# A mixed attention and convolution kernel: value products of two score slots in one operation, V read back per tile, final inputs loaded early and summed in place

## The chip, the cores and the metric

The kernel runs on one core of one Trainium2 chip. The metric is device time in microseconds (us), smaller is better. Its engines are TensorE (PE in the profile, with its weight loads PEld), VectorE (DVE), ScalarE (ACT) and GpSimd (POOL); SyncE (SP) issues every DMA of this kernel.

## The reference

Two mixers read the same input x (1 x 2048 x 512, bf16) and a gate blends them:

```
g = sigmoid((x * gate_w).sum(-1))
out = g * A(x) + (1 - g) * B(x)

A: 32 heads of 16, 4 segments of 512 tokens. In each segment
   a_dot = softmax(q k^T / 4 + causal mask) v
   a_mem = phi(q) M / (phi(q) z + 1e-6),   phi(t) = t + 1 if t > 0 else exp(t)
   o = sigmoid(beta) * a_mem + (1 - sigmoid(beta)) * a_dot
   M += phi(k)^T v,  z += sum phi(k)         (after the segment)
   A = o @ wo
B: K[d, l] = Re sum_n C dt B exp(dt A l)     (128 states, 2048 lags)
   B = causal convolution of x with K over 2048 tokens, by FFT, + x * D
```

## The kernel before

The kernel is a list of operations that a planner at build time puts into an order for each engine. An operation names its engine, a cost, the tiles that it reads and writes and a key. The planner (`Sched.schedule`, L266) repeatedly lets the engine that can start earliest take, among its operations that are ready within 0.12 us, the one with the lowest key; a copy out of PSUM (`evac`, L254) may go to ACT or DVE, and its key counts `PEN` higher on DVE. DMAs are given a length from their bytes (L251) and stand in SP's list like any operation. On the chip each engine runs its list in order and waits on semaphores. So the keys and costs only set the order; they are written by hand: `KEYS` (L19) spaces the groups of attention, the tables and the tail.

Tiles come from pools at fixed addresses of SBUF. Pools of a later phase lie over those of an earlier one and are given out only when the earlier ones are wholly used up (`blockers`). All eight PSUM banks are shared.

The work, in the order of the keys:

- *Powers* (`ssm_powers`, L800). z = exp(dt A) is squared ten times, so that z^(2^k) exists for k = 0 to 10, each copied to a bf16 tile as re, re, im, -im: two ACT copies (L805, L807), one DVE negation (L809), two ACT squares (L815, L816) and two DVE operations (L817, L818) a level.
- *Attention* (`project`, `group`, `ophase`, `oproj`). For each of 4 segments and 4 head groups of 8 heads there are two `group` calls (L979) of four heads A, B, C, D, 32 in all. A group has five score slots. In a slot PE computes scores transposed, keys on partitions, for two or four (head, key block J) pairs into 1024 columns of two PSUM banks, adds the causal mask by matmuls with an identity, ACT takes the exponential of all 1024 columns (L1012) into a tile `pT`, and PE multiplies it with the values (`g`, L1025). From group `MASKD` on, the mask is a product on DVE instead (L1021). A value product of a head fills 17 of the array's columns, so four heads have a column tile each (`tile_position=(0, 32 * c)`). The slots of A and B and of C and D are separate, except the last one (J = 2), which holds all four heads:

```
slots = [[(Ah, 0, 0, 0), (Bh, 0, 1, 0)],
         [(Ah, 1, 0, 0), (Bh, 1, 1, 0), (Ah, 3, 0, 384), (Bh, 3, 1, 384)],
         [(Ch, 0, 0, 0), (Dh, 0, 1, 0)],
         [(Ch, 1, 0, 0), (Dh, 1, 1, 0), (Ch, 3, 0, 384), (Dh, 3, 1, 384)],
         [(Ah, 2, 0, 0), (Bh, 2, 1, 0), (Ch, 2, 0, 256), (Dh, 2, 1, 256)]]
```

  Block J has 512 - 128 J columns. `ophase` (L1042) transposes and normalizes, `oproj` (L1093) multiplies with wo, scales by the gate and stores rows of the attention part to a scratch tensor `scr_abuf`, 16 stores in all. `gate_tokens` (L878) makes the gate; for the last segment it sends the gate through memory (`scr_gbuf`), and a DVE operation (L896) waits for it.
- *Tables* (`tables`, L1110), four times. Products of the powers (L1138, L1140, L1143) build 20 and 32 factors, whose PE products give the filter K; it goes through memory (`scr_K`).
- *First transform of the convolution input* (`x_level1`), stored to `scr_Z`.
- *Tail* (`tail`, L1192). A loop over 16 tiles t, 3.8 of key apart: the filter's transform, the input's second transform, their complex product on DVE (L1240 to L1244), the inverse transform into V, a copy, and a 256-KB store to `scr_V` (L1258). After every fourth tile 1 MB is read back from it into 32 partitions of `V2` (L1261). Then 16 final sums in four groups of four: a load of x (`xj`) and its product u with D on DVE (L1273), a load of the attention part (`aj`, after all 16 stores of it), three matmuls with an identity and the constant `G2`, and a DVE operation (L1286) that scales, adds `aj` and writes `ou`, which is stored, 512 KB for each group. `xj`, `u`, `aj` and `ou` have two buffers each.

Of the kernel before, what the change touches and what calls it, by code (L numbers as in the profile page):

```python
# [8 lines left out]
BF16 = mybir.dt.bfloat16  # L9
# [6 lines left out]
PEN = 20.0  # L16
MASKD = 24
SHOW = 1
KEYS = (11, 6, 60, 65)  # L19
# [482 lines left out]
def fft_consts():  # L502
# [64 lines left out]
def build_kernel(nc, A_x, A_wq, A_wk, A_wv, A_wo, A_beta, B_A_re, B_A_im, B_B_re, B_B_im,  # L567
                 B_C_re, B_C_im, B_log_dt, B_Dskip, gate_w, out):
    with contextlib.ExitStack() as es:
# [27 lines left out]
        mask01 = cload(pidx[None, :] >= pidx[:, None], "mask01", BF16, 8)  # L597
# [45 lines left out]
        pTP = mkpool("pT", 2048, 7)  # L643
# [12 lines left out]
        pwP = mkpool("pw", 4096, 11)  # L656
# [143 lines left out]
        def ssm_powers(pb, dt, zr, zi):  # L800
            S.tag = "pow"
            A = lambda T: ap(T, n=512)
            for k in range(11):
                pw = Tile(pwP, BF16)
                op("ACT", c_act(1024), lambda e, pw=pw, zr=zr: e.activation(  # L805
                    ap(pw, 0, [[512, 4], [128, 2], [1, 128]]), ap(zr, 0, [[128, 4], [0, 2], [1, 128]]), ACT.Copy), r=[zr], pw=[pw])
                op("ACT", c_act(512), lambda e, pw=pw, zi=zi: e.activation(  # L807
                    ap(pw, 256, [[512, 4], [1, 128]]), ap(zi, 0, [[128, 4], [1, 128]]), ACT.Copy), r=[zi], pw=[pw])
                op("DVE", c_ts4(512), lambda e, pw=pw: e.tensor_scalar(  # L809
                    ap(pw, 384, [[512, 4], [1, 128]]), ap(pw, 256, [[512, 4], [1, 128]]), -1.0, None, ALU.mult), r=[pw], pw=[pw])  # L810
                pws.append(pw)
                if k == 10:
                    break
# [28 lines left out]
        dV = [DT() for _ in range(4)]  # L842
# [136 lines left out]
        def group(s, hg, gi):  # L979
# [3 lines left out]
            slots = [[(Ah, 0, 0, 0), (Bh, 0, 1, 0)],  # L983
                     [(Ah, 1, 0, 0), (Bh, 1, 1, 0), (Ah, 3, 0, 384), (Bh, 3, 1, 384)],
                     [(Ch, 0, 0, 0), (Dh, 0, 1, 0)],
                     [(Ch, 1, 0, 0), (Dh, 1, 1, 0), (Ch, 3, 0, 384), (Dh, 3, 1, 384)],
                     [(Ah, 2, 0, 0), (Bh, 2, 1, 0), (Ch, 2, 0, 256), (Dh, 2, 1, 256)]]
# [3 lines left out]
            seen = {}  # L991
            for si, ent in enumerate(slots):
# [41 lines left out]
                for (hh, J, bk, off) in ent:  # L1034
                    seen[hh] = 1
# [339 lines left out]
```

## Time and profile before

| | |
|---|---|
| three runs, us | 419.36, 419.50, 422.38; median 419.5 |
| the profiled execution | 417.59 us, its span 415.8 us, mean granted clock 0.923 |
| instructions | 8543, of them 3609 matmuls, 589 on DVE, 386 on ACT |
| DMA | 42.06 MB in 41029 packets, mean 101 GB/s |
| longest single waits of engines | PE 12.1 us for `scr_V` at the end; DVE 8.6 us for the gate (L896) |
| wait of ACT's copies (L256) for PE | 54.9 us in 54 waits |

Nearly all matmuls stand under L709, the line of a helper; shapes tell them apart: `128*17` is a value product (128 rows, 17 columns of the array), `32*128` a score product, `128*32 128x20` a table product. L256, L257, L259 and L260 are the copies out of PSUM on ACT and DVE, L252 the DMA issue. A row of a group gives its count, busy time, mean length of one in ns, and the idle time of the engine before it with what ended that.

### The profile page before, as it was taken

What the parts mean: (1) busy time and instruction counts of PE and PEld (TensorE: products, weight loads), DVE (VectorE), ACT (ScalarE), POOL (GpSimd) and SP (SyncE); (2) the same over time, 40 slices, a digit from 0 to 9 for tenths busy, and PEclk for the clock granted to TensorE, in tenths of its full rate; (3) what the DMA queues carried; (4) which work ended last, traced back from release to release, by engine and by line L of the source; (5) the groups of instructions that cost most, each with busy time, mean ns of one, the idle gap of its engine ahead of it and who ended that gap; (6) DMA issues with size and microseconds to landing.
All of it is one profiled execution on the core that took longest, in us unless ns stands there. A gap on an engine that the chain in (4) does not pass through costs nothing.

```text
span 415.8 us, 8543 instructions
## 1 busy us (share of the span) xinstructions
PE 341.9 (82%) x3609; PEld 147.3 (35%) x3609; DVE 310.1 (75%) x589; ACT 297.3 (72%) x386; POOL 3.2 (1%) x9
## 2 busy tenths in 40 slices
PE   4896969899959999999999998488779999982460
PEld 3342313333334543544445442144323334330220
DVE  4889997999547998699953995497626799971283
ACT  4999997988828799889888998299656554841000
POOL 1000000000000000000000000000000000000000
PEclk9998888999979999999999999599889999995595
DMA  8901100021445010010100100156944498577253
GB/s 209 275 31 53 50 0 2 0 77 55 149 121 138 31 52 2 19 18 0 52 2 19 17 2 1 43 216 199 347 121 145 165 253 215 197 198 221 50 150 153
DMA packets 41029, 42.06 MB, mean 101 GB/s; under 512 B 18976, under 2 KB 34464, under 8 KB 40608
## 3 DMA queue, kind: packets, MB, share of 16 engines
q1 hardware_dynamic: 40992, 41.52, 33.8%
q8 instruction: 28, 0.46, 0.5%
q14 instruction: 9, 0.07, 0.1%
HBM read 28.27 MB, written 13.25 MB: 100 GB/s over the span
## 4 chain that ended last, share of the span: by engine, by line
PE 37%; DVE 27%; ACT 19%; DMA 11%; issue 4%; SPq 1%; DVEq 0%
PE psum L709 36%; ACT sb L1012 11%; DVE sb L1143 4%; DVE sb L1140 4%; DVE sb L257 3%; DVE sb L1138 3%; DMA scr_gbuf<-sb 3%; ACT sb L256 2%; DMA sb<-in_A_x_dram 2%; DMA sb<-scr_V 2%; DVE sb L1273 2%; DMA out_dram<-sb 1%; DVE sb L1058 1%; SPq L252 1%; DMA sb<-in_A_wq_dram 1%
## 5 line engine op out<-in xcount | busy, mean ns | idle before, releaser
L709 PE MATMUL psum<-sb 128*32 128x20 bf16 (+13 forms) x3393 | 326.6, 274 | 54.2 <-DMA sb<-scr_V 12.1
L709 PEld LDWEIGHTS psum<-sb 128*32 128x32 bf16 (+4 forms) x3393 | 132.5, 95 | 244.2 <-issue 86.1
L1012 ACT ACTIVATE sb<-psum 128x1024 bf16<-128x1024 f32 x160 | 155.3, 1028 | 11.3 <-PE psum L709 10.4
L256 ACT ACTIVATE sb<-psum 128x512 bf16<-128x512 f32 (+4 forms) x110 | 83.2, 770 | 60.7 <-PE psum L709 54.9
L257 DVE CAST sb<-psum 128x512 bf16<-128x512 f32 (+2 forms) x50 | 45.1, 908 | 36.2 <-PE psum L709 35.7
L1143 DVE TENSOR_TENSOR sb<-sb 128x512 bf16<-128x512 bf16 (+3 forms) x52 | 34.7, 667 | 1.4
L1138 DVE TENSOR_TENSOR sb<-sb 128x512 bf16<-128x512 bf16 (+3 forms) x52 | 35.3, 678 | 0.6
L1140 DVE TENSOR_TENSOR sb<-sb 128x512 bf16<-128x512 bf16 (+3 forms) x52 | 34.9, 672 | 0.0
L1286 DVE SCALAR_TENSOR_TENSOR sb<-psum,sb 128x512 bf16<-128x512 f32 x16 | 11.2, 745 | 19.5 <-PE psum L709 16.2
L259 ACT ACTIVATE sb<-psum,sb 128x512 bf16<-128x512 f32 x27 | 18.3, 691 | 7.2 <-PE psum L709 6.9
L260 DVE TENSOR_SCALAR sb<-psum,sb 128x512 bf16<-128x512 f32 x21 | 15.7, 747 | 4.3 <-PE psum L709 3.5
L1021 DVE TENSOR_TENSOR sb<-sb 128x512 bf16<-128x512 bf16 (+1 forms) x40 | 14.4, 364 | 3.6 <-ACT sb L1012 3.4
L805 ACT ACTIVATE sb<-sb 128x1024 bf16<-128x1024 f32 x11 | 11.7, 1060 | 0.0
L1244 DVE TENSOR_TENSOR sb<-sb 128x1024 bf16<-128x1024 bf16 x16 | 11.1, 692 | 0.6
L1240 DVE TENSOR_TENSOR sb<-sb 128x1024 bf16<-128x1024 bf16 x16 | 11.1, 692 | 0.6
L1058 DVE TENSOR_TENSOR sb<-psum,sb 128x512 bf16<-128x512 bf16 x16 | 11.1, 691 | 0.5
L1242 DVE TENSOR_TENSOR sb<-sb 128x1024 bf16<-128x1024 bf16 x16 | 11.0, 685 | 0.0
L1050 PE MATMUL psum<-sb 128*128 128x128 bf16 x128 | 10.4, 228 | 0.5 <-DVE sb L257 0.2
L1050 PEld LDWEIGHTS psum<-sb 128*128 128x128 bf16 x128 | 8.2, 102 | 4.0 <-ACT sb L256 1.4
L1077 DVE TENSOR_TENSOR sb<-psum,sb 128x256 bf16<-128x256 f32 x24 | 9.1, 419 | 0.3
L1055 DVE RECIPROCAL sb<-psum 128x32 f32<-128x32 bf16 x16 | 5.6, 352 | 4.8 <-PE psum L1050 4.7
L922 DVE TENSOR_SCALAR sb<-psum 128x512 bf16<-128x512 f32 x12 | 8.2, 685 | 1.3 <-ACT sb L921 1.2
(65 smaller groups left out, 143.4 us busy)
## 6 DMA issues: line engine op xcount, KB each, us to landing
sb<-in_A_x_dram SPq DMA_DIRECT2D x12, 512.0 KB, 4.6
sb<-c_D SPq DMA_DIRECT2D x16, 320.0 KB, 3.6
scr_Z<-sb SPq DMA_DIRECT2D x16, 256.0 KB, 2.2
sb<-scr_Z SPq DMA_DIRECT2D x4, 1024.0 KB, 11.1
scr_V<-sb SPq DMA_DIRECT2D x16, 256.0 KB, 2.4
sb<-scr_V SPq DMA_DIRECT2D x4, 1024.0 KB, 7.4
scr_abuf<-sb SPq DMA_DIRECT2D x16, 128.0 KB, 1.9
sb<-scr_abuf SPq DMA_DIRECT2D x4, 512.0 KB, 4.7
```

Source lines behind the costliest of these rows:

```text
L256: fa = lambda e: e.activation(dst(), src(), ACT.Copy)
L257: fd = lambda e: e.tensor_copy(dst(), src())
L259: fa = lambda e: e.activation(dst(), src(), ACT.Copy, scale=scale())
L260: fd = lambda e: e.tensor_scalar(dst(), src(), scale(), None, ALU.mult)
L709: mm = lambda e, o_, l, r_, st, sp, **kw: e.matmul(o_, lhsT=l, rhs=r_, start=st, stop=sp, skip_group_check=True, **kw)
L1012: op("ACT", c_act(1024), lambda e, P=P, pT=pT: e.activation(ap(pT, n=1024), ap(P, n=1024), ACT.Exp, scale=0.25), r=[P], w=[pT])
L1021: op("DVE", c_tt(128 * len(offs)), lambda e, pT=pT, dims=dims: e.tensor_tensor(ap(pT, dims=dims + [[1, 128]]), ap(pT, dims=dims + [[1, 128]]),
L1050: i = e.transpose(ap(P, tb * 256 + gi * 128, n=128), ap(ra[gi], tb * 128, n=128), ap(ident, n=128))
L1058: op("DVE", c_dps(512), lambda e: e.tensor_tensor(ap(o1, dims=[[128, 4], [16, 8], [1, 16]]), ap(P, dims=[[256, 4], [32, 8], [1, 16]]), ap( ...
L1138: op("DVE", c_tt(256 * n), lambda e: e.tensor_tensor(run(tile, ne, dst, 1), run(tile, ne, src, sstep), pwv(0), ALU.mult), r=rd + [pw], w=w ...
L1140: op("DVE", c_tt(256 * n), lambda e: e.tensor_tensor(run(t2, n, 0, 1), run(tile, ne, src, sstep), pwv(1), ALU.mult), r=rd + [pw], w=[t2])
L1143: op("DVE", c_tt(256 * n), lambda e: e.tensor_tensor(D_(), D_(), ap(t2, n * 128, [[-n * 128, 2], [2 * n, 64], [1, 2 * n]]), ALU.add), r=[t ...
```

## The change

The change edits seven things.

1. *Groups.* The five slots become three sets: {A/B block 0, C/D block 0}, {A/B blocks 3 and 1, C/D blocks 3 and 1}, {all heads block 2}. Scores and exponentials stay per slot; both slots of a set write halves of one tile (`pT2`, three buffers; the single tile has one), and there is one mask product and one value operation a set. Its matmuls are sorted so that four heads follow each other. Block 3 now lies ahead of block 1 in its bank.
2. *V.* Every tile is read back by itself after its store: 256 KB into 8 partitions, 16 apart. The rows of `G2` are permuted to match.
3. *Final inputs.* `xj` and `aj` have four buffers each; u is written over `xj`, the sum over its quarter of `aj`; the last group is stored in two halves.
4. *Powers.* Ten levels instead of eleven; the two table steps that used z^1024 are made with z^512 from other factors, the second from the first's result. The copies may go to either engine, and level 0 copies only re and im.
5. *Mask.* `MASKD` 24 becomes 25, so group 24 is masked by matmuls.
6. *Planner.* `PEN` 20 becomes 6.53.
7. *Keys.* New spacings: groups 11 to 11.26, start of attention 6 to 11.5, tables 60 to 60.5 and 65 to 67.9 apart, tail loop 3.8 to 3.16, powers 6 to 10.8, tail start 5 to 43.9 after the tables, `oproj` of a segment from 10 to 16.9 groups after its start.

```diff
-PEN = 20.0
-MASKD = 24
+PEN = 6.53
+MASKD = 25
 SHOW = 1
-KEYS = (11, 6, 60, 65)
+KEYS = (11.26, 11.5, 60.5, 67.9, 3.16, 10.8, 43.9, 16.9)
...
-            G2[4 * tp + i, 0, np.arange(32) * 4 + i] = 2.0 / 4096 * np.cos(ang[:, tp])
-            G2[4 * tp + i, 1, np.arange(32) * 4 + i] = -2.0 / 4096 * np.sin(ang[:, tp])
+            r = 16 * (4 * (tp % 2) + i) + tp // 2
+            G2[r, 0, np.arange(32) * 4 + i] = 2.0 / 4096 * np.cos(ang[:, tp])
+            G2[r, 1, np.arange(32) * 4 + i] = -2.0 / 4096 * np.sin(ang[:, tp])
...
-        pTP = mkpool("pT", 2048, 7)
+        pT2P = mkpool("pT2", 4096, 3)
+        pTP = mkpool("pT", 2048, 1)
...
-        xj2P = mkpool("xj2", 4096, 2, 2)
-        uP = mkpool("u", 4096, 2, 2)
-        ajP = mkpool("aj", 4096, 2, 2)
-        ouP = mkpool("ou", 4096, 2, 2)
+        xj2P = mkpool("xj2", 4096, 4, 2)
+        ajP = mkpool("aj", 4096, 4, 2)
...
-            for k in range(11):
+            for k in range(10):
...
+                if k == 0:
+                    S.evac(lambda pw=pw: ap(pw, 128, [[512, 4], [1, 128]]), lambda zr=zr: ap(zr, 0, [[128, 4], [1, 128]]), 512, r=[zr], pw=[pw], psum16=True)
+                else:
+                    S.evac(lambda pw=pw: ap(pw, 0, [[512, 4], [128, 2], [1, 128]]), lambda zr=zr: ap(zr, 0, [[128, 4], [0, 2], [1, 128]]), 1024,
+                           r=[zr], pw=[pw], psum16=True)
+                S.evac(lambda pw=pw: ap(pw, 256, [[512, 4], [1, 128]]), lambda zi=zi: ap(zi, 0, [[128, 4], [1, 128]]), 512, r=[zi], pw=[pw], psum16=True)
+                if k > 0:
+                    op("DVE", c_ts4(512), lambda e, pw=pw: e.tensor_scalar(
+                        ap(pw, 384, [[512, 4], [1, 128]]), ap(pw, 256, [[512, 4], [1, 128]]), -1.0, None, ALU.mult), r=[pw], pw=[pw])
                 pws.append(pw)
-                if k == 10:
+                if k == 9:
...
+            sets = [[[(Ah, 0, 0, 0), (Bh, 0, 1, 0)], [(Ch, 0, 0, 0), (Dh, 0, 1, 0)]],
+                    [[(Ah, 3, 0, 0), (Bh, 3, 1, 0), (Ah, 1, 0, 128), (Bh, 1, 1, 128)],
+                     [(Ch, 3, 0, 0), (Dh, 3, 1, 0), (Ch, 1, 0, 128), (Dh, 1, 1, 128)]],
+                    [[(Ah, 2, 0, 0), (Bh, 2, 1, 0), (Ch, 2, 0, 256), (Dh, 2, 1, 256)]]]
+            mdims = [[[1024, 2], [512, 2], [1, 128]], [[1024, 2], [512, 2], [1, 256]], [[512, 2], [256, 2], [1, 128]]]
...
+            for si, slots in enumerate(sets):
+                pT = Tile(pT2P if len(slots) == 2 else pTP, BF16)
+                for sj, ent in enumerate(slots):
...
+                    op("ACT", c_act(1024), lambda e, P=P, pT=pT, sj=sj: e.activation(ap(pT, sj * 1024, n=1024), ap(P, n=1024), ACT.Exp, scale=0.25),
+                       r=[P], pw=[pT])
...
+                def g(e, pT=pT, slots=slots, si=si):
+                    ents = [(sj, en) for sj, ent in enumerate(slots) for en in ent]
+                    ents.sort(key=lambda x_: -x_[1][1] if si == 0 else (x_[1][1] != 1))
+                    for sj, (hh, J, bk, off) in ents:
                         c = hh % 4
                         n = 512 - 128 * J
                         i = mm(e, ap(PV, 128 * J, n=n, p0=32 * c, np_=17), ap(vpad[s], J * 544 + (8 * hg + hh) * 17, n=17),
-                               ap(pT, bk * 512 + off, n=n), hh not in sn, J == 2, tile_position=(0, 32 * c))
-                        sn[hh] = 1
+                               ap(pT, sj * 1024 + bk * 512 + off, n=n), si == 0, si == 2, tile_position=(0, 32 * c))
                     return i
-                for (hh, J, bk, off) in ent:
-                    seen[hh] = 1
-                op("PE", 0.32, g, r=[pT, vpad[s]], pw=[PV], key=S.key + 2.5, acq=[raw] if si == 0 else [])
+                op("PE", (0.34, 0.36, 0.24)[si], g, r=[pT, vpad[s]], pw=[PV], key=S.key + 2.5, acq=[raw] if si == 0 else [])
...
-            fm(16, 7, 4, 2, 10)
-            fm(18, 13, 2, 2, 10)
+            fm(16, 13, 2, 2, 9)
+            fm(18, 16, 1, 2, 9)
...
-                S.key = k0 + 4 + 3.8 * t
+                S.key = k0 + 4 + KEYS[4] * t
...
-                S.dma(lambda t=t: bass.AP(Vd, t * 131072, [[1024, 128], [1, 1024]]), lambda V=V: ap(V, n=1024), 262144, r=[V], pw=[dV[t // 4]])
-                if t % 4 == 3:
-                    k = t // 4
-                    S.dma(lambda k=k: ap(V2, n=16384, p0=32 * k, np_=32), lambda k=k: bass.AP(Vd, k * 524288, [[16384, 32], [1, 16384]]),
-                          1 << 20, r=[dV[k]], pw=[V2])
+                S.dma(lambda t=t: bass.AP(Vd, t * 131072, [[1024, 128], [1, 1024]]), lambda V=V: ap(V, n=1024), 262144, r=[V], pw=[dV[t]])
+                S.dma(lambda t=t: sbp(V2, t, 16, 8, [[1, 16384]]), lambda t=t: bass.AP(Vd, t * 131072, [[16384, 8], [1, 16384]]),
+                      262144, r=[dV[t]], pw=[V2], packets=1680)
...
+                u = xj
+                op("DVE", c_f1(2048), lambda e, u=u: e.tensor_tensor(ap(u, dims=[[512, 4], [1, 512]]), ap(u, dims=[[512, 4], [1, 512]]),
+                                                                   ap(dskbT, dims=[[0, 4], [1, 512]]), ALU.mult), r=[dskbT], w=[u], key=k0 + 45)
...
-                    op("DVE", c_dps(512), lambda e, P=P, ou=ou, aj=aj, bl=bl, b4=b4: e.scalar_tensor_tensor(
-                        ap(ou, bl * 512, n=512), ap(P, n=512), ap(omg4T, b4, n=1), ap(aj, bl * 512, n=512), ALU.mult, ALU.add),
-                        r=[P, aj, omg4T], pw=[ou])
-                S.dma(lambda gq=gq: bass.AP(out, gq * 2048, [[8192, 128], [1, 2048]]), lambda ou=ou: ap(ou, n=2048), 524288, r=[ou])
+                    op("DVE", c_dps(512), lambda e, P=P, aj=aj, bl=bl, b4=b4: e.scalar_tensor_tensor(
+                        ap(aj, bl * 512, n=512), ap(P, n=512), ap(omg4T, b4, n=1), ap(aj, bl * 512, n=512), ALU.mult, ALU.add),
+                        r=[P, omg4T], w=[aparts[bl]])
+                nh = 2 if gq == 3 else 1
+                for hh in range(nh):
+                    m = 4 // nh
+                    S.dma(lambda gq=gq, hh=hh, m=m: bass.AP(out, gq * 2048 + hh * m * 512, [[8192, 128], [1, 512 * m]]),
+                          lambda aj=aj, hh=hh, m=m: ap(aj, hh * m * 512, n=512 * m), 524288 // nh, r=aparts[hh * m:hh * m + m])
...
-        S.key = 6.0
+        S.key = KEYS[5]
...
-            S.key = TA0 + GA * (8 * s + 10)
+            S.key = TA0 + GA * (8 * s + KEYS[7])
...
-        tail(TT0 + 4 * TT + 5)
+        tail(TT0 + 4 * TT + KEYS[6])
```

More of the change, by code (lines that the diff above doesn't have):

```diff
@@ L841, in build_kernel @@
         dA = [DT() for _ in range(16)]
-        dV = [DT() for _ in range(4)]
+        dV = [DT() for _ in range(16)]
         dK = [DT() for _ in range(4)]
@@ L1271, in tail @@
                       524288, r=dA, w=[aj], key=k0 + 50)
[L1272 to L1275 removed]
+                u = xj
+                op("DVE", c_f1(2048), lambda e, u=u: e.tensor_tensor(ap(u, dims=[[512, 4], [1, 512]]), ap(u, dims=[[512, 4], [1, 512]]),
+                                                                   ap(dskbT, dims=[[0, 4], [1, 512]]), ALU.mult), r=[dskbT], w=[u], key=k0 + 45)
+                aparts = [aj.part() for _ in range(4)]
+                for a_ in aparts:
+                    a_.wr = list(aj.wr)
                 for bl in range(4):
@@ L1298, in build_kernel @@
         gates()
-        GA, TA0, TT0, TT = KEYS
+        GA, TA0, TT0, TT = KEYS[:4]
         for s in range(4):
```

77 lines of the change are left out of this document (26 added, 51 removed).

## The prediction

> **What bounds the kernel now.** I read the page first, then busy time by stage, then the end of the chain of waits. Page, section 1 (busy us, share of the span, instructions):
>
> ```profile
> PE 341.9 (82%) x3609; PEld 147.3 (35%) x3609; DVE 310.1 (75%) x589; ACT 297.3 (72%) x386; POOL 3.2 (1%) x9
> ```
>
> Busy time by stage (after the stretch and its length: PE, weight loads, DVE, ACT, POOL, granted clock, DMA share, GB/s):
>
> ```profile
> 0.00:308.44 308.44, 262.87 (x3181) 117.58 (x3182) 241.60 (x488) 258.25 (x346) 3.19 (x9) 0.94 0.26 75
> ...
> 20.00:40.00 20.00, 15.82 (x143) 7.42 (x142) 18.48 (x40) 19.88 (x32) 0.00 (x0) 0.95 0.15 52
> 40.00:60.00 20.00, 15.50 (x92) 5.18 (x91) 19.65 (x38) 19.81 (x29) 0.00 (x0) 0.84 0.08 27
> ...
> 160.00:180.00 20.00, 19.44 (x399) 9.95 (x400) 14.47 (x37) 16.65 (x26) 0.67 (x1) 1.00 0.10 17
> 180.00:200.00 20.00, 19.54 (x187) 8.96 (x186) 19.51 (x33) 18.36 (x25) 0.00 (x0) 1.00 0.06 17
> 200.00:220.00 20.00, 18.98 (x230) 9.22 (x227) 13.67 (x34) 17.16 (x21) 0.00 (x0) 1.00 0.04 14
> 220.00:240.00 20.00, 19.77 (x376) 9.78 (x372) 14.27 (x32) 18.42 (x26) 0.00 (x0) 1.00 0.12 19
> ...
> 308.44:378.84 70.40, 66.70 (x380) 25.04 (x380) 53.07 (x83) 39.04 (x41) 0.00 (x0) 0.96 0.65 190
> 378.84:389.80 10.96, 0.00 (x0) 0.00 (x1) 0.00 (x0) 0.00 (x0) 0.00 (x0) 0.50 0.72 205
> 389.80:410.74 20.94, 12.31 (x48) 4.63 (x48) 15.40 (x18) 0.00 (x0) 0.00 (x0) 0.83 0.38 125
> ```
>
> There are four parts. Until 308 us the score groups and the tables run, with PE, ACT and DVE all within 22 us of each other, and the limit changes: ACT at 20 to 60, PE at 160 to 240. Then comes the convolution loop, 70 us on PE; then 11 us in which no engine works; then 21 us of final sums. The end of the chain (start, us, what) says what those last two parts wait for:
>
> ```profile
> 377.79 1.03 ACT sb L256
> ...
> 378.84 3.73 DMA scr_V<-sb
> ...
> 382.58 7.17 DMA sb<-scr_V
> ...
> 389.80 3.70 PE psum L709 x9
> ...
> 394.21 2.27 DVE sb L1273
> 396.47 0.67 DVE sb L1286
> 397.14 0.02 issue
> 397.16 2.83 DMA sb<-scr_abuf
> 399.99 1.99 DVE sb L1286 x3
> ...
> 402.36 5.63 DMA out_dram<-sb
> ```
>
> The last V tile is stored, a quarter of V comes back in one 1-MB read, and the sums then stall on a late product with D, a late load of the attention part and an output store that still holds the buffer.
>
> **The change part by part.** The profiled execution took 417.6 us, of which its span is 415.8; the sum is made against 417.6. The median of the three times shown, 419.5, stands 1.9 above it, and the forecast is given at the median's level.
>
> *Value products.* Five stretches, each one run of value products up to the next matmul's start (the count includes one neighbour at the edge); the first number after the length is PE's time:
>
> ```profile
> 30.12:30.45 0.32, 0.32 (x3) 0.09 (x3) 0.32 (x2) 0.32 (x1) 0.00 (x0) 1.00 0.00 0
> 105.14:105.47 0.33, 0.33 (x7) 0.10 (x7) 0.00 (x0) 0.33 (x1) 0.00 (x0) 1.00 0.85 234
> 139.69:140.23 0.54, 0.54 (x7) 0.20 (x7) 0.51 (x2) 0.54 (x2) 0.00 (x0) 1.00 0.00 0
> 112.51:112.83 0.32, 0.32 (x5) 0.11 (x6) 0.29 (x2) 0.22 (x1) 0.00 (x0) 1.00 0.70 253
> 49.67:49.89 0.22, 0.22 (x5) 0.10 (x6) 0.22 (x1) 0.22 (x1) 0.00 (x0) 1.00 0.00 0
> ```
>
> In order: two heads of 512 alone 0.32; two of 512 with two other heads' 384 and 128 0.33; the same six of only two heads 0.54; four of 384 and 128 on two heads 0.32; four heads of 256 0.22. The second against the third is the heart of it: four column tiles share the time, two do not. Today a group has two products of 512, two of 384 and 128, and one of 256: 4 x 0.32 + 0.22 = 1.50 us if each stands alone, 2 x 0.54 + 0.22 = 1.30 where neighbours on the same heads follow each other. I take the smaller. Changed: all four heads' 512 in 0.32, all four's 384 and 128 in 0.32, and 0.22: 0.86. That is 0.44 us a group and 14.1 us of PE over 32 groups. How much of it reaches the end? Up to 308 us PE (262.9) is ahead of ACT (258.3) by only 4.6. PE is at 19 of 20 us or more only at 160 to 240, a third of the groups' time; elsewhere the saving becomes PE idle time. I take 6.0, somewhat under half. It cannot give more than 14.1. It can also lose: a product now waits for two exponentials, and PE's waits on them, 7.6 us today, might double.
>
> ```profile
> PE psum L709 <- ACT sb L1012: 7.6, 16, 1.5
> DVE sb L896 <- DMA sb<-scr_gbuf: 8.6, 1, 8.6
> ...
> L1012 ACT ACTIVATE sb<-psum 128x1024 bf16<-128x1024 f32 x160 | 155.3, 1028 | 11.3 <-PE psum L709 10.4
> L805 ACT ACTIVATE sb<-sb 128x1024 bf16<-128x1024 f32 x11 | 11.7, 1060 | 0.0
> L807 ACT ACTIVATE sb<-sb 128x512 bf16<-128x512 f32 x11 | 7.0, 633 | 0.0
> L815 ACT ACTIVATE sb<-sb 128x512 f32<-128x512 f32 x10 | 6.3, 628 | 0.0
> ```
>
> *Powers.* One level fewer takes from ACT 1.06 (L805), 0.63 (L807) and two squares of 0.63 (L815 and its twin), 2.95 us; the first level's copy shrinks from 1.06 to 0.63, another 0.43: 3.4 in all. They lie at 20 to 60 us, where ACT is busy 19.9 and 19.8 of 20. DVE is at 18.5 and 19.7 there, so copies that may now go to DVE find little room. I take 2.5, between 0 (hidden) and 3.4 with the 1.7 that DVE loses too (5.1). The table products change exponents but not number or size: 0.
>
> *Masks, order.* One group fewer is masked on DVE and instead needs ten identity matmuls on PE, at 0.1 to 0.2 us 1 to 2 us; DVE gains about as much; 0, bounds 2 either way. The new keys and the lower handicap of DVE in the planner reorder everything; no row prices that. The largest price of one bad place is DVE's 8.6 us on the gate's round trip through memory (L896), whose code and place in the plan stay. I take 0 and 8 either way.
>
> *Attention's output projection of the last segment* gets a key behind the final sums, so PE does it only when it has nothing else: up to 16 matmuls of 512, at 0.26 (142.2 us over 545, row below) 4.2 us, leave the full loop for the 11-us hole. But then the attention part is stored and loaded late. I take 1.5, bounds 4.2 gain and 4 loss.
>
> ```profile
> L709 PE MATMUL psum<-sb 128*128 128x512 bf16 x545 | 142.2, 404 | 24.1 <-DMA sb<-scr_V 12.1 <-issue 5.1 <-DVE sb L257 2.5
> L1286 DVE SCALAR_TENSOR_TENSOR sb<-psum,sb 128x512 bf16<-128x512 f32 x16 | 11.2, 745 | 19.5 <-PE psum L709 16.2 <-DMA out_dram<-sb 3.3
> L1273 DVE TENSOR_TENSOR sb<-sb 128x2048 bf16<-128x2048 bf16 x4 | 9.0, 2282 | 0.0
> ...
> scr_V<-sb SPq DMA_DIRECT2D x16, 256.0 KB, 2.4
> sb<-scr_V SPq DMA_DIRECT2D x4, 1024.0 KB, 7.4
> scr_abuf<-sb SPq DMA_DIRECT2D x16, 128.0 KB, 1.9
> sb<-scr_abuf SPq DMA_DIRECT2D x4, 512.0 KB, 4.7
> out_dram<-sb SPq DMA_DIRECT2D x4, 512.0 KB, 4.4
> ```
>
> *Readback.* 1 MB took 7.17 at the end. A tile is a quarter, but its eight rows are as long as the 32 rows before, so a row's own time stays. Between 2.4 (256 KB, 128 rows) and 7.4 (1 MB) I take 4.6, near the 512-KB loads: gain 2.5, bounds 4.8 and 0. SP issues 16 readbacks instead of 4, each waiting some 2.4 us for its store; behind it stand the next constant loads, which have four buffers, and V stores, which have five: 0 with that cover, a few us without.
>
> The Trainium skill ("DMA: Bandwidth & Descriptors", on how many engines a transfer uses) says that a transfer over eight partitions runs on eight of the sixteen engines, and to keep all sixteen busy. That speaks against this shape, and no row above shows it; spread over sixteen, the readback would be near the 2.4 and the sum about 2 us lower.
>
> *Final sums.* 20.94 us now. With products and attention parts ready and results written in place, the three stalls go. What is left is the first block's three matmuls, 1.2 us (3.70 over 9 at the low clock), 16 sums at 0.70 (11.2 over 16), and 1.0 because the next two blocks' matmuls are as slow and outlast a sum by 0.5 each; with 0.3 for the steps between, 13.7, a gain of 7.2. Bounds: all 15.4 that DVE is busy today stay, 5.5; only PE's 12.3, 8.6. Two products with D of 2.28 each move into the loop, where DVE has 17 us free (53.1 of 70.4): 0; without that cover 4.6. The last store is half as large (4.4 toward 2.4): 0.4, bounds 0 and 2.
>
> Sum: 6.0 + 2.5 + 1.5 + 2.5 + 7.2 + 0.4 = 20.1; 417.6 - 20.1 = 397.5, at the median's level **399.4**. A cross-check up to 308 us: if ACT is the busiest afterwards with 254.9 us, and the busiest keeps today's share (262.9 of 308.4, 85%), that part takes 299, a gain of 9.4 against the 8.5 assumed.
>
> **The rivals.** (a) *Only the end gains.* For it: three engines lie close together up to 308 us, and each waits for the others. Against: PE is full at 160 to 240. Gain 2.5 + 7.2 + 0.4: 419.5 - 10.1 = 409.4. (b) *PE is the bound throughout.* For it: 82% on the page and the whole loop. Then 14.1 of the products, 2.5 of the powers, 4.2 of the projection and 10.1 of the end: 388.6. (c) *The attention part comes late.* After the last loop matmul: 4.2 of projection, 0.7 for its last copy (as long as a sum), 1.9 for the store and 4.7 for a load, 11.5; V is there after 1.0 + 2.4 + 4.6 = 8.0. Four loads of 4.7 then share the queue. If the last sums wait 5 us: 404.4. (d) *Slower: the pairing starves PE.* Each of 64 paired sets waits for a second exponential of 1.03 us. If w of it is uncovered on average, 64w is added; from w = 0.31 the 20.1 are gone. At w = 0.5 the time is 399.4 + 32 = 431.4. For it: the pairs' buffers number three, so PE can run ahead only so far. Against: PE waits on exponentials only 7.6 us today, with tables, projections and convolution input to fill in. (e) *The columns do not overlap*, so the change does not do what it says: 405.4; against it stands the 0.33 run.
>
> **How the numbers follow.** Forecast 0.52, (a) 0.17, (b) 0.15, (c) 0.08, (d) 0.05, (e) 0.03. The range must reach into (b) and over (a): 386 to 411 leaves out (d) and tails of (a) and (b), about 0.15. All but (d) and the far side of (a) are faster by more than 1% (1% is about what a measurement of this kernel can tell from no change): faster 0.90, within 1% 0.05, slower 0.05.
>
> **What would show it.** Right: the four-head 512 run takes about 0.32; PE busy falls by 12 to 15 us; the last readback lands in 4 to 5 us; from V's landing to the last sum 13 to 15 us with no wait on a store or a load; L805 to L816 have one level fewer. The 8.6-us wait on the gate's round trip is still there. Wrong: PE's waits on L1012 well over 8 us (d); the groups and tables ending at 308 us as before (a); the sums waiting for the attention part (c); a new stall of DVE or PE of several us from the reordering.

## The result and the profile after

| | before | changed |
|---|---|---|
| runs, median us (lowest to highest) | 420.6 (419.4 to 422.4), 4 runs | 395.2 (389.8 to 398.9), 4 runs |
| ratio to before, 95% interval | | 0.931 (0.923 to 0.939) |
| the same kernel, a second time | 418.8 (414.2 to 425.3), 19 runs | 393.0 (390.0 to 398.4), 4 runs |
| its ratio | | 0.942 (0.929 to 0.955) |

The forecast was 399.4, range 386 to 411: the sign, the size and the range held, and the gain was somewhat larger than the sum. Some executions ran at a lower granted clock and took longer, the changed kernel's first profiled one among them (span 397.0 at 0.886), so the ratios leave these out and the profile read here is of another (span 388.2 at 0.912, 390.0 us of device time).

Section 1 of its page, then busy time by stage (columns as in the prediction: PE, weight loads, DVE, ACT, POOL, granted clock, DMA share, GB/s):

```profile
PE 330.6 (85%) x3619; PEld 144.3 (37%) x3619; DVE 311.3 (80%) x579; ACT 287.8 (74%) x369; POOL 3.2 (1%) x9
```

```profile
0.00:291.20 291.20, 249.12 (x3155) 112.66 (x3155) 241.54 (x475) 244.80 (x324) 3.15 (x9) 0.91 0.26 77
20.00:40.00 20.00, 14.74 (x122) 6.81 (x120) 18.62 (x34) 19.75 (x33) 0.00 (x0) 0.83 0.07 23
40.00:60.00 20.00, 14.87 (x123) 5.96 (x125) 18.05 (x41) 18.12 (x27) 0.00 (x0) 0.74 0.03 3
...
291.24:359.09 67.85, 66.45 (x413) 25.71 (x410) 58.86 (x88) 40.66 (x44) 0.00 (x0) 1.00 0.70 206
360.14:368.72 8.58, 0.74 (x5) 0.13 (x3) 0.00 (x0) 1.29 (x2) 0.00 (x0) 0.72 0.56 156
368.72:382.91 14.19, 13.21 (x48) 5.28 (x48) 10.90 (x16) 0.00 (x0) 0.00 (x0) 0.81 0.64 250
```

PE is busy 11.3 us less than before (341.9 on the page shown in the prediction). The four parts are still there: groups and tables, now to 291; a loop of 68 us on PE; a hole of 8.6 us; final sums of 14.2 us, which PE, busy 13.2 of them, now paces, and no longer DVE (10.9). The end of the chain of waits (start, us, what) has lost the waits on loads and stores:

```profile
359.09 1.03 ACT sb L256
360.14 3.34 DMA scr_V<-sb
...
363.50 5.18 DMA sb<-scr_V
...
368.72 6.11 PE psum L709 x15
374.92 1.91 DVE sb L1281 x3
...
379.54 2.72 DVE sb L1281 x4
```

Where the 27.6 us of span came from, by four points of the two traces: the last copy of the loop starts at 359.1 instead of 377.8 (18.7); from there to V's landing it takes 9.6 instead of 12.0 (2.4); the sums take 14.2 instead of 20.9 (6.7); the rest after the last sum is 0.2 longer. The 18.7 splits again at the last exponential, which is L1012 before (duration min/median/max in ns, first and last start). The second fence is one of the two squares of the powers, same view, same kernel:

```profile
L1012 ACT ACTIVATE sb<-psum x160: 1000/1024/1107, 24.0 to 306.0; 128x1024 bf16<-128x1024 f32 x160
```

```profile
L815 ACT ACTIVATE sb<-sb x10: 612/622/651, 22.5 to 57.9; 128x512 f32<-128x512 f32 x10
```

The same square after the change; the last exponential starts at the end of the first row above, at 291.2:

```profile
L818 ACT ACTIVATE sb<-sb x9: 617/631/701, 21.0 to 46.7; 128x512 f32<-128x512 f32 x9
```

Up to the last exponential the gain is 14.8 (306.0 to 291.2), in the loop behind it 3.9. And the last square starts 11.2 us earlier, for one level less.

### The profile page after: what moved, and what is told of

Read it like the earlier page. It is cut to its first block, busy times and chain, and to the rows that moved or that the text cites. A ratio compares the mean times of both kernels' runs of the same rounds, so it can differ in the third digit from the quotient of the medians.

```text
span 397.0 us, 8521 instructions
## 1 busy us (share of the span) xinstructions
PE 334.2 (84%) x3578; PEld 146.6 (37%) x3619; DVE 311.6 (78%) x579; ACT 288.6 (73%) x369; POOL 3.2 (1%) x9
## 4 chain that ended last, share of the span: by engine, by line
PE 50%; DVE 22%; DMA 12%; ACT 10%; issue 3%; SPq 1%; DVEq 0%; ACTq 0%
PE psum L709 48%; ACT sb L1015 5%; DVE sb L257 4%; DMA sb<-in_A_x_dram 4%; DVE sb L1138 3%; DMA scr_gbuf<-sb 3%; DVE sb L1135 3%; DVE sb L1133 3%; ACT sb L256 2%; DVE sb L1281 2%; PE psum L1045 2%; DMA sb<-in_A_wq_dram 1%; DMA sb<-scr_V 1%; SPq L252 1%; DMA scr_abuf<-sb 1%
## 5 line engine op out<-in xcount | busy, mean ns | idle before, releaser
L709 PE MATMUL psum<-sb 128*32 128x20 bf16 (+12 forms) x3362 | 317.0, 283 | 50.2 <-DVE sb L1019 8.4
L709 PEld LDWEIGHTS psum<-sb 128*128 128x128 bf16 (+4 forms) x3403 | 131.0, 98 | 232.3 <-issue 106.2
L256 ACT ACTIVATE sb<-psum 128x1024 bf16<-128x1024 f32 (+4 forms) x103 | 81.7, 808 | 42.3 <-PE psum L709 36.6
L257 DVE CAST sb<-psum 128x512 bf16<-128x512 f32 (+2 forms) x60 | 50.6, 845 | 32.2 <-PE psum L709 31.6
L259 ACT ACTIVATE sb<-psum,sb 128x512 bf16<-128x512 f32 x30 | 20.7, 690 | 4.9 <-PE psum L709 3.5
L1281 DVE SCALAR_TENSOR_TENSOR sb<-psum,sb 128x512 bf16<-128x512 f32 x16 | 10.9, 745 | 12.6 <-DMA sb<-scr_abuf 12.5
L260 DVE TENSOR_SCALAR sb<-psum,sb 128x512 bf16<-128x512 f32 x18 | 13.4, 746 | 2.5 <-PE psum L709 1.8
L1045 PE MATMUL psum<-sb 128*128 128x128 bf16 x128 | 11.5, 242 | 0.8 <-ACT sb L259 0.5
L1019 DVE TENSOR_TENSOR sb<-sb 128x512 bf16<-128x512 bf16 (+1 forms) x21 | 10.3, 501 | 2.1 <-ACT sb L1015 2.1
L256 ACT ACTIVATE sb<-sb 128x512 bf16<-128x512 f32 (+2 forms) x21 | 11.3, 578 | 0.3
L1237 DVE TENSOR_TENSOR sb<-sb 128x1024 bf16<-128x1024 bf16 x16 | 10.9, 684 | 0.0
L1266 DVE TENSOR_TENSOR sb<-sb 128x2048 bf16<-128x2048 bf16 x4 | 9.1, 2284 | 0.0
```

The source lines that it names most:

```text
L256: fa = lambda e: e.activation(dst(), src(), ACT.Copy)
L257: fd = lambda e: e.tensor_copy(dst(), src())
L259: fa = lambda e: e.activation(dst(), src(), ACT.Copy, scale=scale())
L260: fd = lambda e: e.tensor_scalar(dst(), src(), scale(), None, ALU.mult)
L709: mm = lambda e, o_, l, r_, st, sp, **kw: e.matmul(o_, lhsT=l, rhs=r_, start=st, stop=sp, skip_group_check=True, **kw)
L1045: i = e.transpose(ap(P, tb * 256 + gi * 128, n=128), ap(ra[gi], tb * 128, n=128), ap(ident, n=128))
```

## The experiments

Twelve runs, in three groups of four, each group beside runs of the kernel before on the same chip. Ratios are to that kernel; the interval is 95%.

### The end alone, the groups alone, and a late gate

**The changed kernel unaltered.** 

> The changed kernel unaltered, for a second profile. Theory: the profile of the changed kernel shows PE at a lower granted clock in stretches where it is busy (0.65 at 40 to 60 us, 0.71 at 80 to 100 us), and that alone makes its span 397; a profile with a clock over 0.90 shows a span of 388 to 392 and the group part ending 5 to 8 us sooner, the part from V's landing to the last sum unchanged at 12.3 us. Rival: the shorter runs differ by a wait (a DMA), then the clock is the same and one wait is shorter by 7 to 9 us.

Measured: 393.0, ratio 0.942 (0.929 to 0.955), given above. Its profile is the one read here. The span and the clock came as expected, and the last exponential starts even 9.3 us sooner than in the first profiled execution (300.5); but the sums took 14.2 us and not 12.3, with PE busy 13.2 of them at a granted clock of 0.81. In it a value run of four heads' 512, one of 384 and 128, and one of 256:

```profile
187.43:187.75 0.32, 0.32 (x5) 0.09 (x5) 0.32 (x2) 0.32 (x2) 0.00 (x0) 1.00 0.00 0
202.58:202.91 0.33, 0.33 (x9) 0.11 (x9) 0.22 (x1) 0.31 (x1) 0.00 (x0) 1.00 0.00 0
203.46:203.68 0.22, 0.22 (x6) 0.10 (x5) 0.00 (x0) 0.11 (x1) 0.00 (x0) 1.00 0.00 0
```

Four heads take what two took: 0.32, 0.33 and 0.22, where the forecast had 0.32, 0.32 and 0.22. Its waits (us in total, times, longest):

```profile
DVE sb L1281 <- DMA sb<-scr_abuf: 13.1, 1, 13.1
DVE sb L899 <- DMA sb<-scr_gbuf: 8.9, 1, 8.9
...
PE psum L709 <- ACT sb L1015: 8.5, 16, 1.5
```

PE waits for exponentials 8.5 us instead of 7.6, in the same 16 waits: the pairing does not starve it. The gate's round trip stays. The first row is DVE's idle time in the hole, put down to the last thing that came: the first load of the attention part landed at 371.0, V at 368.7 and the first block's three matmuls a good microsecond later, so that the sums waited about 1 us for that load, not 13. Even that 1 us did not move the end: PE did its 48 matmuls from 368.7 on without a pause.

**The new end in the kernel before.** Tile-wise readback, final inputs in place with four buffers, last store in halves; groups, powers and order as before.

```diff
-        xj2P = mkpool("xj2", 4096, 2, 2)
-        uP = mkpool("u", 4096, 2, 2)
-        ajP = mkpool("aj", 4096, 2, 2)
-        ouP = mkpool("ou", 4096, 2, 2)
+        xj2P = mkpool("xj2", 4096, 4, 2)
+        ajP = mkpool("aj", 4096, 4, 2)
...
+                S.dma(lambda t=t: sbp(V2, t, 16, 8, [[1, 16384]]), lambda t=t: bass.AP(Vd, t * 131072, [[16384, 8], [1, 16384]]),
+                      262144, r=[dV[t]], pw=[V2], packets=1680)
```

> The kernel before with only the edits of V's readback and of the final inputs and sums; groups, powers, masks, handicap and keys stay. Theory: the end's gain is its own, 10 to 12 us: 408 to 410 against 420.6, with the readback near 5 us, V's landing to the last sum near 12.5 us, and the part up to 308 us unchanged. Rival: the end needs the new order (projection behind the loop, later start of the tail); then the gain is under 6 us: 415 or more.

Measured: 422.2, ratio 1.005 (0.999 to 1.011): nothing. The end of its chain:

```profile
360.60 8.81 DVE sb L1270 x4
...
385.09 13.77 DMA sb<-scr_V
398.90 2.76 PE psum L708 x6
```

The last readback takes 13.77 us instead of 5.18. With four buffers all four loads of the attention part, 2 MB, are issued ahead of the last two readbacks and share the engines with them. And the four products with D (L1270) come in a row, 8.8 us of DVE near the end of the loop. What the sums gain is given back before they start.

**The three sets in the kernel before.** Only the groups of the change.

```diff
-            slots = [[(Ah, 0, 0, 0), (Bh, 0, 1, 0)],
...
+            sets = [[[(Ah, 0, 0, 0), (Bh, 0, 1, 0)], [(Ch, 0, 0, 0), (Dh, 0, 1, 0)]],
...
+                pT = Tile(pT2P if len(slots) == 2 else pTP, BF16)
```

> The kernel before with only the groups' edit (three sets for five slots, one value operation a set); end, powers, handicap, MASKD and keys stay. Theory of the forecast: about 6 us less, 412 to 416, since half of PE's 14 us lies beside ACT's and DVE's work. Rival one, PE bounds throughout: 12 to 15 us less, 406 to 409. Rival two, the pairing starves PE and only the new order repairs it: 420 or more, with PE's waits on L1012's exponentials over 12 us.

Measured: 416.6, ratio 0.996 (0.993 to 0.9995). Its page, then PE between 60 and 90 us, and one shorter stretch of it:

```profile
PE 343.1 (83%) x3609; PEld 146.3 (35%) x3609; DVE 308.6 (75%) x574; ACT 299.5 (72%) x385; POOL 3.2 (1%) x9
```

```profile
60.00:90.00 30.00, 27.47 (x166) 7.87 (x164) 24.61 (x44) 24.28 (x33) 0.00 (x0) 0.52 0.00 1
...
61.00:71.00 10.00, 10.00 (x54) 2.43 (x52) 9.72 (x21) 8.08 (x11) 0.00 (x0) 0.50 0.01 2
```

The kernel before, same stretch:

```profile
60.00:90.00 30.00, 27.84 (x226) 9.77 (x224) 27.21 (x47) 26.75 (x35) 0.00 (x0) 0.91 0.05 15
```

PE has less to do and is busy 1.2 us more (343.1 to 341.9). It ran at half clock from 58.1 to 88.8: as busy as before, with 166 matmuls done instead of 226. To the end of each loop, before, the changed kernel and this one:

```profile
0.00:377.79 377.79, 329.57 (x3561) 142.63 (x3561) 294.67 (x571) 296.27 (x386) 3.19 (x9) 0.95 0.33 97
```

```profile
0.00:359.09 359.09, 315.61 (x3564) 138.37 (x3565) 300.40 (x563) 285.50 (x367) 3.15 (x9) 0.92 0.35 102
```

```profile
0.00:373.76 373.76, 329.63 (x3561) 141.34 (x3561) 293.14 (x556) 298.43 (x384) 3.18 (x9) 0.88 0.34 97
```

The granted clock is 0.95, 0.92 and 0.88. So what the shorter products saved did not show in PE's busy time: at the lower clock fewer matmuls are done in the same busy time (166 in those 30 us, against 226). The Trainium skill ("TensorE: Matmul & The Clock Gate", Part 1) says that about 3.4 us of sustained activity bring the full clock back; the row from 61.00, by which PE is busy for all of 10.00 us at 0.50, inside 30.7 us at half clock, does not bear that out here (the ends of matmuls are modelled, so short gaps may hide in it). Why the clock stayed low is open.

**The gate's operation moved behind the tables in the changed kernel.** It removes DVE's longest wait ahead of the final sums.

```diff
-                op("DVE", 0.2, lambda e: e.tensor_scalar(ap(omg4T, n=16), ap(g4T, n=16), -1.0, 1.0, ALU.mult, ALU.add), r=[g4T], w=[omg4T])
...
+            op("DVE", 0.2, lambda e: e.tensor_scalar(ap(omg4T, n=16), ap(g4T, n=16), -1.0, 1.0, ALU.mult, ALU.add), r=[g4T, KTT], w=[omg4T], key=k0)
```

> The changed kernel with one operation moved: the DVE operation that waits for the gate's round trip through memory (L899, 8.9 us of DVE wait) stands in the tail, where the gate has long arrived. Theory: DVE, then PE and ACT, stood still for it with nothing else to do, so 6 to 9 us go: 382 to 385 against about 391 in undisturbed runs. Rival: the wait was cover for something else that is late next (SP's own wait of 11 us on the same transfer, the tables' constants behind it), then 0 to 2 us.

Measured: 391.9, ratio 0.940 (0.934 to 0.945), the same as the changed kernel. The 8.9-us wait is gone and the last exponential is 3.7 us earlier (287.5), but the loop's last copy only 0.8 (358.3). Then the end of its chain:

```profile
362.79 7.33 DMA scr_abuf<-sb
370.13 3.99 DMA sb<-scr_abuf
374.14 2.16 DVE sb L1281 x4
```

The sums start at 374.1 instead of 371.0, because the attention part is now stored last and loaded after it: rival (c) of the prediction is what stands right behind the present end.

### Each part undone, and the order by itself

**The old order in the changed kernel, and the new order in the old kernel.**

```diff
-PEN = 6.53
-MASKD = 25
+PEN = 20.0
+MASKD = 24
...
-KEYS = (11.26, 11.5, 60.5, 67.9, 3.16, 10.8, 43.9, 16.9)
+KEYS = (11, 6, 60, 65, 3.8, 6, 5, 10)
```

> The changed kernel with the planner's numbers of before: handicap of DVE 20, MASKD 24, keys 11, 6, 60, 65, loop 3.8, powers 6, tail 5, projection 10; all other edits stay. Theory: groups alone gave 0.4% and the end alone nothing, so the gain hangs on the order: 405 to 415 here, of the 29 us more than half lost, with readbacks piling up behind SP as with the end alone. Rival: the edits carry each other (the groups free PE, so that the end comes in time), then 393 to 400 and the order is worth little.

> The kernel before with only the planner's numbers of the changed kernel (handicap 6.53, MASKD 25, all keys); groups, end and powers stay. Theory that the order carries the part before the loop's end: 10 to 16 us less, 403 to 409, the last exponential near 295. Rival, the order only fits the other edits: 415 to 422.

Measured: the changed kernel in the old order 413.2, ratio 0.980 (0.972 to 0.988); the kernel before in the new order 415.4, ratio 0.985 (0.977 to 0.993). So 3.8 to 4.9 of the hundredths gained hang on the order, which the forecast had put at 0, while the order alone brings 1.5. With the order alone the last exponential starts at 303.4, where 295 was expected. In the changed kernel with the old order it starts at 320.6 and the loop ends at 373.6, 14.5 us later than in the changed kernel; the four products with D stand in the chain (first line), as with the end alone, and the last readback is as slow as there:

```profile
354.63 8.80 DVE sb L1266 x4
...
374.66 4.08 DMA scr_V<-sb
378.76 13.75 DMA sb<-scr_V
```

From those products to the loop's last copy (354.6 to 373.6) PE is busy 15.0 of 19.0 us, so 4.0 are idle. In the changed kernel the same four stand at 301.9 to 322.2, outside the chain, and PE idles 1.4 us in the whole loop. No run moved these products alone. The granted clock over the span is also lower in the old order (0.884 against 0.912); how much of the 20 us is that was not separated.

**The five slots back in the changed kernel.** The diff of the three sets, reversed.

```diff
-            sets = [[[(Ah, 0, 0, 0), (Bh, 0, 1, 0)], [(Ch, 0, 0, 0), (Dh, 0, 1, 0)]],
...
+            slots = [[(Ah, 0, 0, 0), (Bh, 0, 1, 0)],
...
+                pT = Tile(pTP, BF16)
```

> The changed kernel with the five slots and five value operations of before (masks by slot too); order, powers and end stay. If the paired products are worth what the forecast took: 6 us more than the changed kernel, 396 to 399. If PE is the bound throughout: 12 to 16 more, 403 to 407. If the granted clock gives the saving back (groups alone had the clock lowered for 58 us of full-speed time against 33 before): 0 to 3 more, and less time at the low clock than the changed kernel.

Measured: 402.9, ratio 0.957 (0.950 to 0.965): 1.5 to 2.6 hundredths worse than the changed kernel's two ratios, 6 to 11 us. Here the products are worth what the forecast took (6.0) or more, at nearly the same granted clock (0.909 and 0.912); in the kernel before they were worth 0.4 hundredths.

**The old end back in the changed kernel.**

```diff
-        xj2P = mkpool("xj2", 4096, 4, 2)
-        ajP = mkpool("aj", 4096, 4, 2)
+        xj2P = mkpool("xj2", 4096, 2, 2)
+        uP = mkpool("u", 4096, 2, 2)
+        ajP = mkpool("aj", 4096, 2, 2)
+        ouP = mkpool("ou", 4096, 2, 2)
...
+                if t % 4 == 3:
+                    k = t // 4
+                    S.dma(lambda k=k: ap(V2, n=16384, p0=32 * k, np_=32), lambda k=k: bass.AP(Vd, k * 524288, [[16384, 32], [1, 16384]]),
+                          1 << 20, r=[dV[k]], pw=[V2])
```

> The changed kernel with the old end: 1-MB readbacks, two buffers each for x, u, the attention part and the output, one store a group; order (with the projection late), groups and powers stay. Theory: the end is worth its 10 us in the new order: 400 to 404, the final sums taking 19 to 21 us again. Rival: its worth depends on the rest and it loses 3 or less, 394 or less.

Measured: 405.4 over four runs (396.8 to 406.3), without a ratio. The profiled execution is the 396.8, with a span of 395.0, 6.8 more than the changed kernel's. From the loop's end to the last sum it takes 33.8 instead of 23.8 (10.0), with the sums at 22.7 (20.9 in the kernel before) and the store's wait back in the chain:

```profile
380.42 6.76 DMA out_dram<-sb
387.21 0.75 DVE sb L1282
```

But its loop ends 2.9 earlier (356.2). That lies ahead of the loop: its last exponential starts 5.1 earlier (286.1), and the loop itself, with two of the four products with D out of it again, is not shorter (70.1 us at a granted clock of 0.96, against 67.9 at 1.00). The 6.8 rests on one execution of each kernel, so it is rough.

### Three causes, and an attempt at more

**The attention part's loads behind the last readbacks, in the old order.**

```diff
-                      524288, r=dA, w=[aj], key=k0 + 50)
+                      524288, r=dA + [dV[15]], w=[aj], key=k0 + 70)
```

> The run with the old order (all edits, the planner's numbers of before), where the last readback of V took 13.8 us, with one swap in SP's list: the four loads of the attention part (2 MB) come behind the last two readbacks instead of ahead of them. Theory: the readback's eight rows wait behind those 2 MB in the DMA engines, and in the changed kernel the late projection happens to put the loads behind. Then the readback takes 4.5 to 6 us, and the time falls by 4 to 8 us, to 405 to 409. Rival: the long readback is due to readbacks piling up on each other, then 13 to 14 us again and the same time.

Measured: 409.3, ratio 0.973 (0.968 to 0.979). The same place of its chain:

```profile
378.20 8.69 DMA sb<-scr_V
```

The readback falls from 13.75 to 8.69: by these two traces 5.1 of the 8.6 us that it was too long are the loads in front of it. Of these, 2.9 reach the path from the loop's last copy to V's landing (16.1 instead of 18.9), because the last V store is issued and lands later. Another 2.8 of the 6.1 us of span (412.1 to 406.0) lie ahead of that copy and are not explained by the edit; the two ratios' intervals (0.972 to 0.988, 0.968 to 0.979) overlap. What makes the readback still 3.5 too long was not taken apart: two readbacks follow each other, and the loads now come close behind the last one. In the changed kernel the late projection puts the loads behind by itself.

**Eleven levels of powers back in the changed kernel.**

```diff
-            for k in range(10):
+            for k in range(11):
...
+                op("ACT", c_act(1024), lambda e, pw=pw, zr=zr: e.activation(
+                    ap(pw, 0, [[512, 4], [128, 2], [1, 128]]), ap(zr, 0, [[128, 4], [0, 2], [1, 128]]), ACT.Copy), r=[zr], pw=[pw])
```

> The changed kernel with the powers of before: eleven levels, copies on ACT alone, the table steps with z^1024. The forecast took 2.5 us for this edit: 392 to 395 against 389 to 392. Rival: the level is hidden, or the changed order moves more than it costs: within 1.5 us.

Measured: 399.2, ratio 0.946 (0.943 to 0.950), 0.4 to 1.5 hundredths worse than the changed kernel (2 to 6 us), with a span 7.9 longer (396.1). Rows of the changed kernel's powers, 15 to 62 us:

```profile
L256 ACT ACTIVATE sb<-sb 128x512 bf16<-128x512 f32 x11 | 7.0, 636 | 0.2
...
L818 ACT ACTIVATE sb<-sb 128x512 f32<-128x512 f32 x9 | 5.7, 638 | 0.0
...
L257 DVE CAST sb<-sb 128x1024 bf16<-128x1024 f32 x8 | 5.6, 694 | 0.3
...
L256 ACT ACTIVATE sb<-sb 128x1024 bf16<-128x1024 f32 x1 | 1.1, 1057 | 0.1
```

Eight of the nine wide copies now run on DVE, in 0.69 us instead of 1.06. ACT's share of the powers falls from 11.7 + 7.0 + 6.3 + 6.3 = 31.3 us (the rows of L805, L807 and the squares in the prediction) to 7.0 + 1.1 + 5.7 + 5.7 = 19.5. That leaves it time for exponentials. The first 60 us, ACT's exponentials alone (busy, count, clock, DMA share, GB/s), in the changed kernel and with the powers undone:

```profile
0.00:60.00 60.00, 16.96 (x18) 0.86 0.32 91
```

```profile
0.00:60.00 60.00, 11.07 (x11) 0.90 0.39 108
```

Eighteen against eleven; the kernel before has done thirteen. This is the powers' and not the order's: with the new powers it is 16 to 18 in every run (17 in the old order), with the old ones 11 to 13 (12 with the order alone). How much of it reaches the end is less sure. The trace with the powers undone also has the lower granted clock (0.896 against 0.912): from 80 to 100 us PE is as busy in both (19.8 and 19.1) but at 0.50 against 0.98, with 138 matmuls done instead of 182. Which part of the 2 to 6 us is the clock was not separated.

**The old start and spacing of the tail in the changed kernel.**

```diff
-KEYS = (11.26, 11.5, 60.5, 67.9, 3.16, 10.8, 43.9, 16.9)
+KEYS = (11.26, 11.5, 60.5, 67.9, 3.8, 10.8, 5, 16.9)
```

> The changed kernel with two planner's numbers of before: the tail's start 5 instead of 43.9 of key behind the tables, and the loop's spacing 3.8 instead of 3.16. Theory: what the order gives before the loop's end lies here: with the loop's keys ahead of the last groups' the last exponentials come at 315 to 320 as in the run with the old order, beside a loop that cannot go faster, and the time is 8 us or more above the changed kernel, 398 or more. Rival: the handicap of DVE and the groups' spacing carry it, then 389 to 395.

Measured: 401.3, ratio 0.948 (0.941 to 0.954), and the last exponential at 295.3. The two numbers seem to carry a part of the order's price (the interval overlaps that of the changed kernel's 0.942), but not in the way that was expected: the groups do not become late by them (4.1 us, against 29 with the whole old order). Instead the four products with D are back in the chain, as in the old order:

```profile
351.83 2.20 DVE sb L1266
...
356.30 6.61 DVE sb L1266 x3
```

From there to 372.0 PE is busy 15.5 of 20.2 us. So these two numbers decide where those products stand. Which of the other numbers makes the groups late is open.

**The late gate with an early attention part.** An attempt to remove the wait that the late gate had run into.

```diff
-KEYS = (11.26, 11.5, 60.5, 67.9, 3.16, 10.8, 43.9, 16.9)
+KEYS = (11.26, 11.5, 60.5, 67.9, 3.16, 10.8, 43.9, 9)
...
-                      262144, r=[dV[t]], pw=[V2], packets=1680)
+                      262144, r=[dV[t]], pw=[V2], packets=600)
```

> The changed kernel with the gate's DVE operation moved to the tail, as before, and two planner's numbers so that the attention part is stored and loaded well before the loop's end: projection 9 instead of 16.9 groups after the segment's start, a readback's cost 600 instead of 1680 packets. In the run with the late gate alone the group part ended 4 us sooner, but the first sum then waited for the attention part (store 7.3, load 4.0 us) until 374. Theory: with the part already there the sums start right after V, and 4 to 7 us go against the changed kernel: 383 to 387. Rival: the projection, back in the loop, costs its 4 us of PE there, and nothing is left: 388 to 392.

Measured: 415.0, ratio 0.984 (0.981 to 0.988): much worse. The end of its chain, and SP's waits in it and in the changed kernel:

```profile
362.87 5.12 DMA scr_V<-sb
...
368.60 5.32 DMA scr_V<-sb
...
380.73 6.72 DMA scr_V<-sb
387.46 4.94 DMA sb<-scr_V
```

```profile
SPq L252 <- DMA scr_V<-sb: 43.1, 13, 6.3
```

```profile
SPq L252 <- DMA scr_V<-sb: 12.2, 9, 2.5
```

The loop's last copy is at 366.8 (358.3 with the late gate alone), but the last V store is issued only at 380.7. SP's list now holds store, wait for its landing, readback, store, and so on: about 6 us a pair at the end (362.87 to 380.73 for three), against some 3.7 us for a tile of the loop, so that a backlog grows. The readbacks' order, not PE, sets the end. No version was clearly faster than the changed kernel.

## Why the prediction was right, point by point

*Sum.* Of the profiled 417.6 it forecast 397.5 and 390.0 came: 7.5 us more gained. The end was right to about a microsecond (8.9 of 10.1), the body (groups, powers, loop) gave 18.7 instead of 6.0 + 2.5 + 1.5 = 10.0. That the total came within 4 to 6 us of the medians is in part luck: the order, which the sum had at 0, is needed for most of the gain.

*Value products, 6.0: mechanism right, size not general.* Four column tiles do share the time, and PE's busy time fell by 11.3 (forecast 12 to 15). Undone in the changed kernel they cost 6 to 11 us, alone they bring 0.4 hundredths. The term had no place for the clock: with the groups alone a lower granted clock went with the shorter work, as in the stretch from 58 to 89 us above. The stretch in which PE is full was also misread: 160 to 240 is a quarter of 308 us and not a third. In groups undone the loop also starts later on a late readback of the filter, so the whole of its 13.3 us of span is not shown to be the products'.

*Powers, 2.5: mis-sized, and this step failed:* "copies that may now go to DVE find little room". They found room for eight of nine, DVE needing 0.69 for what took ACT 1.06; why DVE had the room is argued, not shown (the stage gets shorter as ACT is relieved, and DVE loses a level too). ACT gained 11.8 us, not 3.4, and the last square starts 11.2 us earlier. At most 2 to 8 us of this reach the end, and some of that may be clock. The cross-check failed for the same reason: it took ACT for the busiest with 254.9 us up to the end of the groups; ACT has 244.8, PE 249.1, and the part takes 291, not 299. The rule in it held: the busiest engine has 86% of the stretch, 85% before.

*Masks and order, 0 with 8 either way.* The order alone gives 1.5 hundredths, within those bounds; but the rest of the change needs it, which no term said. In the old order the changed kernel would have had 413.2, outside the range. The parts do not add: groups 0.4, order 1.5, end -0.5 (powers were not tried alone), and together 6 to 7 hundredths.

*Projection out of the loop, 1.5 with a loss of 4.* The loop behind the last exponential is 3.9 us shorter, but hardly by the projection: only two of its four pieces, 8 of the 16 matmuls, run behind the loop, in 1.8 us. PE's busy time in the loop falls by 0.9 (67.4 to 66.5), its idle time by 3.0 (4.4 to 1.4). Before, two products with D stood in the chain there:

```profile
354.69 4.40 DVE sb L1273 x2
```

In the changed kernel's chain there is none. Neither move was tried by itself. The loss feared, a late attention part, did not come, but lies close by: the sums wait about 1 us for it, and the late gate ran into it.

*Readback, 2.5.* 5.18 at the end where 4.6 was taken, and 2.4 less from the loop's end to V's landing, 2.0 of it in the readback and 0.4 in the store ahead of it: right. "SP issues 16 readbacks ... 0 with that cover, a few us without" was too mild: the waits of SP for these stores are 12.2 us in all here and 43.1 where the cover fails. There the span is 22 us longer than with the late gate alone (412.0 against 390.0): the loop's last copy starts 8.4 later, and the last V store is issued 14.0 after that copy instead of 1.0. The price of the shape itself shows on its neighbours. After, then before:

```profile
sb<-c_D SPq DMA_DIRECT2D x16, 320.0 KB, 6.9
...
scr_V<-sb SPq DMA_DIRECT2D x16, 256.0 KB, 5.4
sb<-scr_V SPq DMA_DIRECT2D x16, 256.0 KB
```

```profile
sb<-c_D SPq DMA_DIRECT2D x16, 320.0 KB, 3.6
```

A V store lands after 5.4 us instead of 2.4, a load of constants after 6.9 instead of 3.6; with the old end in the changed order it is 3.2 and 4.1, so most of this goes with the new end. PE-bound as the loop is, it stays hidden. Each readback shows in the trace as eight packets of 32 KB, 1.4 to 3.5 us each, and none has a landing time in the list. That agrees with the rule quoted in the prediction (the Trainium skill, "DMA: Bandwidth & Descriptors", on how many engines a transfer uses): eight of sixteen.

*Final sums, 7.2, and last store, 0.4.* 14.2 us, where 13.7 was forecast: 6.7, with the three stalls gone. But the 13.7 was built from 16 sums on DVE, and PE sets the pace: 13.2 us for the 48 matmuls at a granted clock of 0.81, where the lower bound had its 12.3. So the size is in part luck. The rest after the last sum is 0.2 longer, so the 0.4 for the last store does not show. The two products with D that moved into the loop cost nothing in the changed order, as forecast, but in the old order the four of them stand in the chain. Net, the new end is worth about 7 in the changed kernel, by one execution of each, and nothing in the kernel before, where the loads that it brings forward delay the readback.

*Rivals.* (a), only the end gains: refuted, the last exponential is at 291, not 306. (b), PE throughout, 388.6: PE is the bound from 291 on and not before (86% to there); the time measured lies between it and the forecast. (c): not in this kernel, next in line. (d) and (e): refuted, by 8.5 us of waits and by the 0.33 runs.

## What to carry to other kernels

A part's value is that of the order it stands in: the same new end was worth some 7 us in the changed kernel and nothing in the kernel before, so a forecast should ask of every load that is brought forward which later transfer it will stand in front of, and of every operation which chain it will stand in. An operation that may go to either engine is priced by what it takes on each and by which engine bounds that stage, not by how full the other one looks. A readback that waits for its own store in an in-order queue needs a distance between the two, or the queue becomes the bound.

## What the hardware showed that was not expected

Half clock with a busy PE: with the groups alone PE ran 30.7 us at 0.50 to 0.52 although it was busy 27.5 of 30, with a stretch of 10 us without a gap in the records. Less PE work did not mean less busy PE: 343.1 us against 341.9. What decides the clock there stays open, and with it how far the groups' gain would carry to another order.
